# Column-half matmuls kept together in groups, and the second batch mixed row by row for all token groups, in a scheduled attention and token-mixing kernel

## Chip, cores and metric

The kernel runs on one core of one Trainium2 chip. The metric is the device time of one execution in microseconds (us). Three executions of the kernel before took 296.97, 297.04 and 297.30 us; the median, 297.04 us, is the time to compare with. The profile comes from one more execution, of 297.23 us, and its span (first to last instruction) is 295.5 us.

## What is computed

The reference has two parts. A polynomial-sketch attention over 4 batches, 4 heads, 1088 tokens and 32 dimensions a head, and then a token-mixing block on the result, laid out as 4 batches of 1088 tokens with 128 features.

```python
def phi(x):                                   # S1, S2: 8 x 32
    a = einsum('rd,bhsd->bhsr', S1, x); b = einsum('rd,bhsd->bhsr', S2, x)
    return outer product of a and b, 64 features for a token and head
q_p, k_p = phi(q), phi(k)
kv  = einsum('bhsf,bhsd->bhfd', k_p, v)       # 64 x 32 for each head
z   = sum of k_p over the tokens
num = einsum('bhsf,bhfd->bhsd', q_p, kv)
den = einsum('bhsf,bhf->bhs', q_p, z) + 1e-6
x = num / den, heads side by side             # (batch, token, 128)

theta = x @ w_theta
zr, zi = x * cos(theta), x * sin(theta)
y = w_tok_r @ zr + w_tok_i @ zi               # over tokens: 1088 x 1088, for each batch
u = x + y
out = u + relu(u @ w_ch)
```

The denominators can come close to zero, so the kernel computes them in slices of numbers that add up exactly (the names `ksl`, `qsl`, `mv`, `lv`, `cut_r`, `cut_z`, `fl` belong to that). The features, `kv`, the numerators and the mixing run on 32-bit floats. The mixing weights come as 64-bit floats and are turned into 32-bit ones on the chip, in 34 pieces (`w_tok` into `st`, then `step` and `wT`).

## The kernel before

The kernel does not call the engines directly. It records each instruction (`note`), with an estimated duration and the earlier instructions that it must follow; at the end `lay_out` goes through a list schedule and issues everything in the order found. Among the instructions of an engine that could start within `WAIT` of the earliest, the one with the smallest `due` is taken. `due` runs back from the mixing matmuls, which get `START[b]` plus a pace, and is shifted for each stage by `SOONER[stage]`. So these constants decide the order on each engine, and the order is fixed when the program is built. Each engine then executes its own list in that order.

```python
START = 101.9, 134.2, 165.1, 246.3
SOONER = {"denominators0": 4.5, "denominators1": -11, ...}     # cut: 49 stages
PACE = 2.9
...
class Order:
    WAIT = 0.08
    ...
    def note(self, engine, fn, call, a, kw):
        ...
        op = Operation(engine, fn, a, kw, len(self.ops), cost, late, self.due)
        op.stage = self.stage
        ...                                    # cut: whom it must follow
        self.ops.append(op)
        return op
    ...
    def lay_out(self):
        ...                                    # cut: the list schedule fills `out`
        for op in out:
            r = [x.real() if isinstance(x, View) else x for x in op.args]
            op.call(*r, **{k: x.real() if isinstance(x, View) else x for k, x in op.kw.items()})
```

PSUM is one pool of 8 buffers of 512 floats a partition, all under the name `w`. Tokens come in 9 chunks of 128 (the last one half filled), and in 3 groups of 3 chunks (`NG = 3`, `GC = 3`). Two places use matmuls whose output has only 64 partitions: a pair of heads gives the columns 0 to 63 of the array, the other pair the columns 64 to 127.

```python
def keys_values(b):                            # feat: features of the keys; big: the values
    vn = tiles["v", b]
    kv = psum()[:, :P]
    for g in range(NG):
        ks = tiles["kf", b, g]
        kp = buf("feat", [P, CH, R, R], F32, 2)
        tt(V, kp, ...)                         # the outer product, on VectorE
        for i in range(GC):
            for n in range(2):
                c = g * GC + i
                T.matmul(kv[n * 2 * D:(n + 1) * 2 * D], vn[:, c, 2 * n:2 * n + 2]...,
                         kp[:, i * H + 2 * n:i * H + 2 * n + 2]...,
                         start=(c == 0), stop=(c == NC - 1),
                         tile_position=(0, n * 2 * D), skip_group_check=True)
    ...                                        # cut: kv is put into kvbd

def numerator(b, g):
    ...                                        # cut: features of the queries, transposed into fT
    xp = psum()[:, :GC * P]
    for n in range(2):
        T.matmul(xp[n * 2 * D:(n + 1) * 2 * D], kvbd[b % 2][:, n], qpT[n],
                 start=True, stop=True, tile_position=(0, n * 2 * D), skip_group_check=True)
    return xp
```

The mixing of a batch adds up 17 products for each group of tokens: 8 chunks of `zr`, 8 of `zi`, and one that holds the two half chunks. The first batch goes row by row: each of the 17 weight rows is used for the three groups at once, as the weights arrive. The other batches go group by group.

```python
rows = [j * NF + i for i in range(NF) for j in range(2)] + [NK - 1]

def mix_sums(b, gs, yps):
    zr, zi, zl = tiles["z", b]
    for n, i in enumerate(rows):
        z = zr[:, i] if i < NF else zi[:, i - NF] if i < NK - 1 else zl
        for g, yp in zip(gs, yps):
            t0, t1 = g * GC * P, min((g + 1) * GC * P, S)
            order.due = START[b] + (PACE * n if len(gs) > 1 else 0.65 * (g * NK + n))
            T.matmul(yp[:, :t1 - t0], z, wT[:, i, t0:t1], start=(n == 0), stop=(n == NK - 1))

def mixing(b):
    for gs in (range(NG),) if b == 0 else ((g,) for g in range(NG)):
        yps = [psum() for _ in gs]
        order.stage = f"mixing{b}"
        mix_sums(b, gs, yps)
        for g, yp in zip(gs, yps):
            mix_out(b, g, yp)                  # add x, the channel matmul, transpose, store
    order.due = math.inf
```

Of the kernel before, what the change touches and what calls it, by code (L numbers as in the profile page):

```python
# [36 lines left out]
ROUND = 1.5 * 2.0**23  # L37
TWO_PI = 6.2831850
TINY = 2.0**-60
START = 101.9, 134.2, 165.1, 246.3  # L40
BIG = 5

SOONER = {"denominators0": 4.5, "denominators1": -11, "denominators2": -106, "denominators3": -89,
          "features0": 23, "features1": 45.5, "features2": -47.5, "features3": 32.5,
          "keyfeatures0": 25, "keyfeatures1": 16.5, "keyfeatures2": 20.5, "keyfeatures3": 67.5,
          "keys1": 45.5, "keys2": -14.5, "keys3": -30.5, "matrix0": 9, "matrix1": 36.5,
          "matrix2": 6.5, "matrix3": 55.5, "mixed00": -8.5, "mixed01": 24.5, "mixed02": -0.5,
          "mixed10": -5, "mixed11": -13, "mixed12": 31, "mixed20": 190, "mixed21": -53,
          "mixed22": 66, "mixed30": 51, "mixed31": 24, "mixed32": -22, "mixing0": -53,
          "mixing1": -66, "mixing2": -52, "mixing3": -24, "out0": -43, "out1": -30, "out2": -26,  # L50
          "out3": 109, "slices0": 3.5, "slices1": -9, "slices2": -72, "slices3": -20, "values0": 5,
          "values1": 39.5, "values2": 28.5, "values3": 17.5}
ST = 6
PACE = 2.9
PIECE = 544


# [54 lines left out]

class Operation:
    def __init__(self, engine, call, args, kw, n, cost, late, due):
        self.engine, self.call, self.args, self.kw, self.n = engine, call, args, kw, n
        self.cost, self.late, self.due = cost, late, due
        self.behind, self.bufs = [], []

# [22 lines left out]
class Order:  # L141
# [3 lines left out]

    WAIT = 0.08

    def __init__(self, nc):  # L150
        self.nc, self.ops, self.due, self.tags, self.stage = nc, [], math.inf, {}, None
        self.dve, self.act = self.Engine(self, "DVE", nc.vector), self.Engine(self, "ACT", nc.scalar)
        self.pe, self.sp = self.Engine(self, "PE", nc.tensor), self.Engine(self, "SP", nc.sync)

# [22 lines left out]
    def duration(self, engine, call, out, ins):  # L177

        n = math.prod(out.shape[1:])
        psum = any(isinstance(x, View) and x.buf.tag == "w" for x in ins)  # L180
        if engine == "DVE":
            if call == "tensor_reduce":
                n = math.prod(ins[0].shape[1:])
            if call == "reciprocal":
                return 0.29, 0.1
            own = any(isinstance(x, View) and x.shape[1:] == (1,) for x in ins[1:])
            fast = call in ("tensor_scalar", "tensor_copy", "memset") and not psum
            return 0.09 + n / (1920 if fast and not own else 1400 if fast else 970), 0.1
        if engine == "ACT":
            wide = any(isinstance(x, View) and x.buf.tag == "st" for x in ins)  # L190
            own = any(isinstance(x, View) and x.shape[1:] == (1,) for x in ins[1:])
            return 0.05 + 0.07 * own + n / (900 if out.dtype != F32 and wide else 1020 if wide else 1130), 0.15
        if engine == "SP":
            return 0.36, 0.0
        if call == "transpose":
            return 0.11, 0.3
        if ins[0].dtype == F32:
            return (n / 1200 + 0.03 if ins[0].shape[1] == 64 else max(0.22, n / 600)), 0.3
        return max(0.06, n / 2400), 0.3

    def note(self, engine, fn, call, a, kw):
        names = [k for k in ("out", "dst") if k in kw]
        out = kw[names[0]] if names else a[0]
        ins = [x for x in [*a, *kw.values()] if x is not out and hasattr(x, "rearrange")]
        cost, late = self.duration(engine, call, out, ins)
        op = Operation(engine, fn, a, kw, len(self.ops), cost, late, self.due)
        op.stage = self.stage
        if engine == "PE":
            passes = 2 if call == "transpose" else 4 if ins[0].dtype == F32 else 1
            op.stream = min(cost, math.prod(out.shape[1:]) * passes / 2400)  # L210
        if engine == "SP":
            op.bytes = math.prod(out.shape) * mybir.dt.size(out.dtype)
        behind = set()
        for x, write in [(x, False) for x in ins] + [(out, True)]:
            if not isinstance(x, View):
                continue
            b = x.buf
            p0, p1, b0, b1 = box = x.box()
            for n, w, (q0, q1, c0, c1) in b.seen:
                if (w or write) and p0 < q1 and q0 < p1 and b0 < c1 and c0 < b1:  # L220
                    behind.add(n)
            if write and engine == "PE":
                if b.pe is not None:
                    behind.add(b.pe)
                b.pe = op.n
            b.seen.append((op.n, write, box))
            if not b.uses or b.uses[-1] != op.n:
                b.uses.append(op.n)
                op.bufs.append(b)
        behind.discard(op.n)  # L230
        op.behind = sorted(behind)
        self.ops.append(op)
        return op

    def dues(self):
# [7 lines left out]
    def lay_out(self):  # L243
# [49 lines left out]
        while len(self.log) < len(ops):  # L293
# [21 lines left out]
            t, op = best  # L315
# [24 lines left out]
                if not left[n]:  # L340
                    ready[o.engine].append(o)
        for op in out:
            r = [x.real() if isinstance(x, View) else x for x in op.args]
            op.call(*r, **{k: x.real() if isinstance(x, View) else x for k, x in op.kw.items()})  # L344


@with_exitstack
def kernel(
# [12 lines left out]
    B, _, NC, H, D = q.shape  # L361
# [4 lines left out]
    NK = 2 * NF + 1  # L366
    GC = 3
    NG = NC // GC
# [334 lines left out]
    def keys_values(b):  # L703
# [5 lines that stand above are left out]
            kp = buf("feat", [P, CH, R, R], F32, 2)  # L709
            tt(V, kp, ks[:, :, 0:R].unsqueeze(3).to_broadcast([P, CH, R, R]),  # L710
               ks[:, :, R:2 * R].unsqueeze(2).to_broadcast([P, CH, R, R]), ALU.mult)
            for i in range(GC):
                for n in range(2):
                    c = g * GC + i

                    T.matmul(kv[n * 2 * D:(n + 1) * 2 * D], vn[:, c, 2 * n:2 * n + 2].rearrange("p h d -> p (h d)"),
                             kp[:, i * H + 2 * n:i * H + 2 * n + 2].rearrange("p h i j -> p (h i j)"),
                             start=(c == 0), stop=(c == NC - 1), tile_position=(0, n * 2 * D), skip_group_check=True)
        kvt = buf("kvt", [P, P])
        A.copy(kvt, kv)  # L720
        t = psum()[:, :P]
        T.transpose(t, kvt, ident)
        t = t.rearrange("p (n d) -> p n d", n=2)
        for j in range(2):
            pj = slice(j * R * R, (j + 1) * R * R)
            A.copy(kvbd[b % 2][pj, :, j * D:(j + 1) * D], t[pj, :, j * D:(j + 1) * D])
# [90 lines left out]
    def numerator(b, g):  # L817
        fl = tiles["fl", b].rearrange("p t (n r) -> p t n r", r=R)[:, :, g * CH:(g + 1) * CH]
        qp = buf("feat", [P, CH, R, R], F32, 2)
        tt(V, qp, fl[:, 1].unsqueeze(3).to_broadcast([P, CH, R, R]),  # L820
           fl[:, 0].unsqueeze(2).to_broadcast([P, CH, R, R]), ALU.mult)
        qpT = [buf("fT", [P, GC * P], F32, 4) for _ in range(2)]
        for n in range(2):
            tr = psum()
            for i in range(GC):
                T.transpose(tr[:, i * P:(i + 1) * P],
                            qp[:, i * H + 2 * n:i * H + 2 * n + 2].rearrange("p h i j -> p (h i j)"), ident)
            A.copy(qpT[n], tr[:, :GC * P])
        xp = psum()[:, :GC * P]
        for n in range(2):  # L830

            T.matmul(xp[n * 2 * D:(n + 1) * 2 * D], kvbd[b % 2][:, n], qpT[n],
                     start=True, stop=True, tile_position=(0, n * 2 * D), skip_group_check=True)
        return xp

    def mixed(b, g, xp):
# [36 lines left out]
# [3 lines that stand above are left out]
            z = zr[:, i] if i < NF else zi[:, i - NF] if i < NK - 1 else zl  # L876
            for g, yp in zip(gs, yps):
                t0, t1 = g * GC * P, min((g + 1) * GC * P, S)
                order.due = START[b] + (PACE * n if len(gs) > 1 else 0.65 * (g * NK + n))
                T.matmul(yp[:, :t1 - t0], z, wT[:, i, t0:t1], start=(n == 0), stop=(n == NK - 1))  # L880

    def mix_out(b, g, yp):
# [29 lines left out]

    def mixing(b):

        for gs in (range(NG),) if b == 0 else ((g,) for g in range(NG)):
            yps = [psum() for _ in gs]
            order.stage = f"mixing{b}"
            mix_sums(b, gs, yps)
# [132 lines left out]
```

## Time and profile before

| | |
|---|---|
| time, median of three | 297.04 us |
| span of the profile | 295.5 us, 3773 instructions |
| TensorE matmul (PE) | 257.6 us busy, 87% |
| VectorE (DVE) | 224.8 us, 76% |
| ScalarE (ACT) | 166.0 us, 56% |
| mean granted TensorE clock | 0.912 |
| read from and written to memory | 28.5 MB, 97 GB/s over the span |

The same, by stretches of time (busy us of each engine, and the granted TensorE clock in that stretch):

| stretch, us | PE | DVE | ACT | clock |
|---|---|---|---|---|
| 0 to 20 | 7.65 | 15.87 | 12.51 | 0.87 |
| 20 to 77 | 37.15 | 55.87 | 45.10 | 0.71 |
| 77 to 140 | 62.49 | 58.85 | 52.74 | 0.90 |
| 140 to 152 | 11.84 | 11.21 | 11.59 | 1.00 |
| 152 to 290 | 137.39 | 82.50 | 43.49 | 1.00 |
| 290 to 296 | 1.05 | 0.49 | 0.53 | 0.91 |

How to read the names: every instruction is issued from the same line of the recording layer (L344), so groups are told apart by their tiles. `w<-wT,st` is a mixing matmul, `w<-feat,big` one of `keys_values` and `w<-fT,kvbd` one of `numerator`; `128*64` means a weight operand of 64 columns. A matmul on 32-bit floats leaves two records in the trace, a transpose or a 16-bit matmul one. The records of one engine overlap: a matmul's record ends after the next one has begun. The room that a matmul takes is therefore read from its start to the start of the next one, not from its length.

### The profile page before, as it was taken

How to read it: one execution, taken by the hardware profiler on the slowest of the kernel's cores; microseconds unless marked ns; L12 is line 12 of the kernel's file. 1: busy time of each engine (PE TensorE's matmuls, PEld its weight loads, DVE VectorE, ACT ScalarE, POOL GpSimd, SP SyncE). 2: the span in 40 equal slices, each digit the busy share in tenths (PEclk: the TensorE clock that was granted, in tenths of full speed). 3: DMA queues.
4: the chain of work that ended last, by engine and by line, in shares of the span. 5: the costliest groups of instructions: out<-in, count | busy, mean ns of one | idle time of the engine just before them, and what ended most of it. 6: DMA issues, size and time to landing. Idle time of an engine off the chain costs nothing.

```text
span 295.5 us, 3773 instructions
## 1 busy us (share of the span) xinstructions
PE 257.6 (87%) x1255; PEld 168.1 (57%) x1255; DVE 224.8 (76%) x638; ACT 166.0 (56%) x326; POOL 0.7 (0%) x6
## 2 busy tenths in 40 slices
PE   4539584945599999999999999999999999999993
PEld 3426553524477656656565545677656666665671
DVE  5999999999998999979999447999881994421011
ACT  3696579999528999789992223226734004620000
POOL 0000000000000000000000000000000000000000
PEclk9957867775559999999999999999999999999999
DMA  7999115967002166753300000110000001000010
GB/s 252 384 355 353 21 67 201 332 239 226 0 0 83 31 205 220 223 151 106 131 1 27 27 2 0 41 36 1 23 2 0 27 0 29 22 0 0 27 29 22
DMA packets 11603, 28.77 MB, mean 97 GB/s; under 512 B 1216, under 2 KB 5568, under 8 KB 11584
## 3 DMA queue, kind: packets, MB, share of 16 engines
q1 hardware_dynamic: 11584, 28.53, 28.7%
q8 instruction: 10, 0.16, 0.2%
q14 instruction: 9, 0.07, 0.1%
HBM read 26.30 MB, written 2.23 MB: 97 GB/s over the span
## 4 chain that ended last, share of the span: by engine, by line
PE 74%; DVE 15%; ACT 7%; DMA 1%; issue 1%; ACTq 0%
PE w L344 74%; ACT step L344 3%; DVE big L344 2%; DVE wT L344 2%; DVE lv L344 2%; DMA big<-k_l 1%; ACT big L344 1%; DVE cut_r L344 1%; DVE ksl L344 1%; DVE feat L344 1%; ACT lv L344 1%; ACT wT L344 1%; ACT tn L344 1%; DVE cut_z L344 1%; ACT fT L344 1%
## 5 line engine op out<-in xcount | busy, mean ns | idle before, releaser
L344 PE MATMUL w<-wT,st 128*128 128x384 f32 (+1 forms) x384 | 130.9, 473 | 0.0
L344 PEld LDWEIGHTS w<-wT,st 128*128 128x128 f32 x384 | 68.3, 190 | 36.9 <-issue 5.2
L344 ACT ACTIVATE step<-st 128x544 f16<-128x544 f32 (+2 forms) x70 | 54.4, 827 | 5.7 <-DVE wT L344 5.6
L344 ACT COPY ot<-w 128x384 f32<-128x384 f32 (+2 forms) x16 | 6.0, 394 | 62.6 <-PE w L344 50.4
L344 DVE TENSOR_TENSOR uT<-xT,w 128x384 f32<-128x384 f32 (+1 forms) x12 | 6.4, 530 | 28.0 <-PE w L344 27.9
L344 PE MATMUL w<-feat,big 128*64 128x128 f32 x144 | 18.3, 325 | 7.5 <-DVE feat L344 7.5
L344 DVE CUSTOM_DVE_ANT_0 wT<-wT,step 128x1088 uint16<-128x1088 uint16 x34 | 24.3, 719 | 0.7 <-ACT step L344 0.3
L344 ACT ACTIVATE wT<-st 128x544 f32<-128x544 f32 x34 | 23.6, 713 | 0.4 <-DMA st<-w_tok 0.4
L344 ACT COPY fT<-w 128x384 f32<-128x384 f32 x36 | 16.2, 490 | 9.9 <-PE w L344 9.9
L344 ACT COPY lv<-w 128x384 f32<-128x384 f32 x36 | 16.1, 500 | 8.3 <-PE w L344 8.0
L344 PEld LDWEIGHTS w<-feat,big 128*64 128x64 f32 x144 | 11.1, 156 | 15.1 <-DVE feat L344 8.2
L344 PE MATMUL w<-ident,big 128*128 128x128 f32 x72 | 13.8, 346 | 6.7 <-ACT big L344 4.2
L344 PE MATMUL w<-s_bd,fT 128*128 128x64 f32 x72 | 13.7, 353 | 6.1 <-DVE s_bd L344 6.1
L344 PE MATMUL w<-mv,qsl 128*128 128x384 f16 (+2 forms) x108 | 16.2, 290 | 1.6 <-ACT lv L344 1.3
L344 PEld LDWEIGHTS w<-s_bd,fT 128*128 128x128 f32 x72 | 12.7, 264 | 6.9 <-DVE s_bd L344 6.2
L344 PEld LDWEIGHTS w<-ident,big 128*128 128x128 f32 x72 | 11.5, 185 | 8.4 <-ACT big L344 4.6
L344 DVE TENSOR_SCALAR wT<-wT 128x544 int32<-128x544 int32 x34 | 14.5, 435 | 0.4 <-ACT wT L344 0.3
L344 PE MATMUL w<-ksl 128*128 128x384 f16 x72 | 14.6, 362 | 0.0
L344 PEld LDWEIGHTS <-qsl 128*128 128x128 f16 x108 | 9.9, 99 | 7.8 <-issue 4.5
L344 PE MATMUL w<-fT,kvbd 128*64 128x384 f32 x48 | 13.3, 542 | 0.2 <-ACT fT L344 0.2
L344 DVE SCALAR_TENSOR_TENSOR tt<-tn,w 128x384 f32<-128x384 f32 x12 | 6.6, 552 | 8.6 <-ACT tn L344 8.4
L344 PE MATMUL w<-ident,feat 128*128 128x128 f32 x72 | 12.9, 302 | 0.3 <-ACT big L344 0.3
(190 smaller groups left out, 402.1 us busy)
## 6 DMA issues: line engine op xcount, KB each, us to landing
st<-w_tok SPq DMA_DIRECT2D x34, 544.0 KB, 4.9
big<-k_l SPq DMA_DIRECT2D x4, 576.0 KB, 4.9
big<-q_l SPq DMA_DIRECT2D x4, 576.0 KB, 3.9
big<-v_l SPq DMA_DIRECT2D x4, 576.0 KB, 5.4
out<-ot SPq DMA_DIRECT2D x8, 192.0 KB, 2.1
out<-ot SPq DMA_DIRECT2D x4, 128.0 KB, 1.8
st<-w_sq SPq DMA_DIRECT2D x1, 256.0 KB, 4.9
out<-ot SPq DMA_DIRECT2D x4, 32.0 KB, 1.8
```

The lines of the kernel that those rows point to most:

```text
L344: op.call(*r, **{k: x.real() if isinstance(x, View) else x for k, x in op.kw.items()})
```

## The change

The change keeps certain instructions together and then sets the scheduler's constants anew.

- `together` makes one operation of all that is recorded inside it. Its parts are issued one after the other with nothing between them, under one estimated cost. It is used for the 6 half matmuls of one group in `keys_values`, and for the 2 of `numerator`, so that instructions on columns 0 to 63 and 64 to 127 alternate and no instruction of another kind stands between them.
- The second batch (`b == 1`) is mixed like the first, row by row for the three groups of tokens, and no longer group by group.
- `START`, `SOONER`, `PACE` and `WAIT` are new, and so are some estimates of `duration`. These are numbers of the scheduler alone, but through them nearly the whole order changes on all engines.

What is computed stays the same. The built program has the same 856 matmul instructions of the same shapes on TensorE as before, and the same number of instructions on VectorE and ScalarE; only their order and the buffers they use differ.

```diff
-START = 101.9, 134.2, 165.1, 246.3
+START = 118, 121.6, 209.9, 242.1
-SOONER = {"denominators0": 4.5, "denominators1": -11, ...}
+SOONER = {"denominators0": 43.5, "denominators1": -128, ...}      # cut: all stages are new
-PACE = 2.9
+PACE = 1.6
-    WAIT = 0.08
+    WAIT = 0.03
...
-            return (n / 1200 + 0.03 if ins[0].shape[1] == 64 else max(0.22, n / 600)), 0.3
+            return max(0.22, n / 600), 0.3
+    @contextmanager
+    def together(self, cost):
+        self.joined = []
+        yield
+        op, self.joined = self.joined[0], None
+        op.cost = cost
...                                            # cut: note() adds to the joined operation
-            op.call(*r, **{k: x.real() if isinstance(x, View) else x for k, x in op.kw.items()})
+            for call, args, kw in op.parts:
+                r = [x.real() if isinstance(x, View) else x for x in args]
+                call(*r, **{k: x.real() if isinstance(x, View) else x for k, x in kw.items()})
...                                            # keys_values
-            for i in range(GC):
-                for n in range(2):
-                    T.matmul(kv[...], ...)
+            with order.together(0.81):
+                for i in range(GC):
+                    for n in range(2):
+                        T.matmul(kv[...], ...)
...                                            # numerator
-        for n in range(2):
-            T.matmul(xp[...], ...)
+        with order.together(0.85):
+            for n in range(2):
+                T.matmul(xp[...], ...)
...                                            # mix_sums
-                order.due = START[b] + (PACE * n if len(gs) > 1 else 0.65 * (g * NK + n))
+                order.due = START[b] + (PACE if b == 0 else 1.95) * n if len(gs) > 1 else START[b] + 0.65 * (g * NK + n)
...                                            # mixing
-        for gs in (range(NG),) if b == 0 else ((g,) for g in range(NG)):
+        for gs in (range(NG),) if b < 2 else ((g,) for g in range(NG)):
```

## The prediction, made before the changed kernel ran

> **What bounds the kernel now.** I read the page from the top: busy times, the span in slices, the chain of waits, then the groups.
>
> ```profile
> PE 257.6 (87%) x1255; PEld 168.1 (57%) x1255; DVE 224.8 (76%) x638; ACT 166.0 (56%) x326; POOL 0.7 (0%) x6
> ...
> PE   4539584945599999999999999999999999999993
> ...
> DVE  5999999999998999979999447999881994421011
> ACT  3696579999528999789992223226734004620000
> ...
> PEclk9957867775559999999999999999999999999999
> ...
> PE 74%; DVE 15%; ACT 7%; DMA 1%; issue 1%; ACTq 0%
> ...
> L344 PE MATMUL w<-feat,big 128*64 128x128 f32 x144 | 18.3, 325 | 7.5 <-DVE feat L344 7.5
> L344 PE MATMUL w<-fT,kvbd 128*64 128x384 f32 x48 | 13.3, 542 | 0.2 <-ACT fT L344 0.2
> ```
>
> A slice is 7.4 us. Up to slice 10 (77 us) VectorE is full and TensorE has holes at a low clock; from there TensorE is full to the end, and the chain is 74% TensorE. VectorE stays nearly full to slice 20 (150 us): it converts the mixing weights beside its other work. So there are three stages: VectorE sets 20 to 77 us; from 77 to about 152 us both are full; from 152 us TensorE alone sets the pace (137.39 of 138 us busy, VectorE 82.50).
>
> Next the timeline of TensorE, for what a column-half matmul costs by its neighbours:
>
> ```profile
> 51.59 0.88 PE L344 MATMUL w<-feat,big 128*64 128x128 f32 x12 [2.52 <-DVE feat L344]
> 52.40 0.96 PE L344 MATMUL w<-ksl 128*128 128x384 f16 x3
> ...
> 128.16 0.86 PE L344 MATMUL w<-fT,kvbd 128*64 128x384 f32 x2
> 128.96 0.83 PE L344 MATMUL w<-ksl 128*128 128x256 f16 x5
> ...
> 174.40 0.43 PE L344 MATMUL w<-feat,big 128*64 128x128 f32 x2
> 174.76 0.27 PE L344 MATMUL w<-ident,m 128*8 128x128 f32 x1
> 174.97 0.43 PE L344 MATMUL w<-feat,big 128*64 128x128 f32 x2
> 175.33 0.91 PE L344 MATMUL w<-wT,st 128*128 128x384 f32 x2
> 176.17 0.43 PE L344 MATMUL w<-feat,big 128*64 128x128 f32 x2
> ...
> 209.54 0.87 PE L344 MATMUL w<-fT,kvbd 128*64 128x384 f32 x4
> 210.34 0.18 PE L344 MATMUL w<-sz,cz 128*128 128x16 f16 x1
> ```
>
> Take starts, not lengths. Six key matmuls in one run (12 records) take 51.59 to 52.40: 0.81 us, 0.135 each. One alone (2 records) takes 174.97 to 175.33: 0.36. The mixing matmul behind it takes 175.33 to 176.17, 0.84, where 0.645 is usual between its own kind: of those 0.19 us, 0.10 follow the half matmul before it and 0.09 precede the next one. One numerator matmul takes 0.80 (128.16 to 128.96), and two together also 0.80 (209.54 to 210.34).
>
> **What the Trainium skill says.** "TensorE: Matmul & The Clock Gate", section Part 3: Packing small matmuls, says that outputs on distinct column strips run at once; the trace agrees, two numerator matmuls in the 0.80 us of one. "TensorEngine Tiling (Array Packing)", section Key Properties, says "Mode switching requires drain": going from whole array to halves empties TensorE. The trace agrees with the 0.09 us before and about 0.10 us behind a run. "Perfetto Trace Analysis", section Identifying the Most-Contended Engine, warns that matmul busy share is no measure of TensorE's room; hence I sum start-to-start steps.
>
> **The change, part by part.**
>
> *Halves together.* Only runs after 77 us count, where TensorE is full. Batch 2's key matmuls (91 to 100.5 us) come in 8 runs of 1 to 3 instructions: their steps sum to 3.75 us, plus 8 entries x 0.09 = 4.5. As 3 whole groups: 3 x (0.81 + 0.09) = 2.7; **1.8 saved**. Batch 3's (162 to 181 us) come in 12 runs among mixing matmuls: 4.8, plus 12 x 0.09, plus about 9 exits into mixing x 0.10 = 6.8; whole: 2.7 + 3 x 0.10 = 3.0; **3.8 saved**. Four numerator matmuls ran alone (128 to 143 us), each 0.80 + 0.09; as two pairs they cost half: **1.8 saved**. The sum is 7.4 us. Nothing is added: the 856 matmuls are the same.
>
> *The order.* The order of the built instructions of both programs is known. I gave each TensorE instruction its full-clock step from the trace (0.645 us for 384 mixing columns, 0.538 for 320, 0.109 a transpose, runs of halves as above) and summed along each order: 230.5 us before, 222.3 after, **8.2 less**. Against the trace, the clock time is this sum plus an offset: 52.5 at the first numerator (86.0 us), 54.4 at 91 us, 55.9 at 152 us, 59.3 at the end. The offset grows by cold clock, idle time and small extra steps; it hardly grows after 90 us, so the sum is a fair ruler.
>
> Likewise for VectorE, mean step of each kind of instruction. Before, it has done 79 us of work at the first query product (83 us); in the new order 81 us stand ahead of it. So the first numerator comes about 2 us later, at 88 us, with 33.1 us of TensorE work ahead of it (before 33.4): offset 55, and 57 after the cold start that before too cost 2 us.
>
> *Mixing batch 1 by rows.* It adds no matmul. It lets this mixing start as soon as the first tokens' `z` are there. In the new order mixing of batch 0 ends at TensorE sum 80 (before 99), batch 1 starts at 90 and ends at 129.
>
> *Where VectorE holds it.* The last row of batch 0's mixing needs the last weights. Before, VectorE had 143 us of work ahead of the end of the last conversion, which ended at 151.4 us; in the new order 133. VectorE had done 133 at 140.1 us. ScalarE's share: its last weight copy ends at its work sum of 112.9, before 120.4 (150.3 us); at 113 it stood near 142 us. So the last weights come at about **141 us**. TensorE's sum is 79 there, so the offset is 62, not 57: TensorE must wait some 4 to 5 us between 120 and 141. Batch 1's first `z` says the same: 144.7 of VectorE work, about 152 us, with TensorE at 90: offset 62. Before, at 152 us, TensorE's sum was 96 of 230.5, leaving 134.5; after it is 90 of 222.3, leaving 132.3. From there the offset grew by 3.4 before, of which I take off about 1.2 for batch 3's fragments: 2.2. End: 222.3 + 62 + 2.2 = 286.5, before 230.5 + 59.3 = 289.8. **3.3 us less**: 297.04 - 3.3 = 293.7. I say 293.4, as order and scheduler were tuned together and a little of the wait may go.
>
> **The rivals.**
>
> *A. TensorE stays the bound all through.* Then offset 57 at 91 us plus 4 gives 222.3 + 61 = 283.3, 6.5 less, 290.5 us. For it: before, TensorE waited only 0.4 us between 86 and 290 us. Against it: VectorE has 58.85 of 63 us busy from 77 to 140 us, and the new order leaves TensorE less other work to put in while weights arrive.
>
> *B. The gain is lost ahead of 77 us.* The order there is new too. VectorE's chain to the first denominators has 64 us of work ahead instead of 62, and a lost handshake between VectorE, ScalarE and TensorE costs 1 to 4 us (before, one wait for `ACT big` was 4.22 us). All later work shifts: 294 to 297.
>
> *C. PSUM runs short.* Three buffers of 8 are held by batch 1's mixing from sum 90 to 129, where one was held before. Work of batches 2 and 3 must go through 5. Batch 0 was mixed with three held and TensorE did not starve (0 idle from 90 to 126 us), so I give this little: 295 if it bites.
>
> *D. A late chain.* The denominators of batch 3 must be done between features (sum 159) and numerators (178) : 19 us, as before (167 to 186), where it just fitted. Slack of 3 to 4 us for batch 2 (113 to 131). A miss costs 1 to 3 us.
>
> **Range and chances.** The middle is 293.4. A brings it to 290.5, B to D to 295 to 297; ordered engines can go wrong in small ways that only a run shows. Range 289.0 to 296.8. 2% faster is 291.1: it needs nearly all of A, chance 0.26. Slower by 2% (303) would need 10 us of new waits: 0.04. The rest, 0.70, lies within 2%.
>
> **What would show it.** The timeline after must show `w<-feat,big` in 12s and `w<-fT,kvbd` in 4s, their steps near 0.81 and 0.80: else the 7.4 us are wrong. TensorE's idle time between 100 and 145 us, waiting for VectorE `wT` or `st`, should be 4 to 6 us; if it is under 1, A holds. The last weight conversion should end near 141 us, the first numerator start near 88. After 152 us TensorE should have under 2 us idle; waits there for `fT`, `z` or a PSUM buffer would speak for C or D. The prediction fails if VectorE reaches 133 us of work clearly before 138 or after 145 us.

## The result and the profile after

| | before | after |
|---|---|---|
| time, median (lowest to highest) | 297.14 us (296.97 to 297.30) | 292.16 us (291.87 to 292.38) |
| ratio, with its 95% interval | 1 | 0.983 (0.9815 to 0.9849) |
| span of the profile | 295.5 us | 290.1 us |
| mean granted TensorE clock | 0.912 | 0.903 |

The changed kernel is 1.7% faster: inside the range and within 2%, 1.2 us under the figure of the prediction. The page of the kernel after, in the order in which the prediction read the page before (busy times, slices, chain, and the group of half matmuls that is among its costliest):

```profile
PE 248.8 (86%) x1255; PEld 165.2 (57%) x1255; DVE 225.6 (78%) x638; ACT 163.5 (56%) x326; POOL 0.7 (0%) x6
...
PE   4699857470049999999999999999999999999993
...
DVE  5999899999999999998999669989862993511011
ACT  3598759999039999999567082037704004710000
...
PEclk9957955865557999999999999999999999999998
...
PE 70%; DVE 20%; ACT 6%; DMA 1%; issue 1%; ACTq 0%
...
L361 PE MATMUL w<-feat,big 128*64 128x128 f32 x144 | 10.5, 281 | 1.8 <-DVE feat L361 1.8
```

The key matmuls fell from 18.3 to 10.5 us busy. Two slices of TensorE (65 to 80 us) and one of ScalarE (72 to 80 us) are now empty; behind them TensorE is full to the end. The timeline of TensorE shows the halves in whole groups (start, length, then what runs; the step to the next start is the cost):

```profile
104.16 0.88 PE L361 MATMUL w<-feat,big 128*64 128x128 f32 x12
104.97 2.20 PE L361 MATMUL w<-wT,st 128*128 128x384 f32 x6
...
137.99 1.99 PE L361 MATMUL w<-wT,z 128*128 128x384 f32 x6
...
142.31 0.87 PE L361 MATMUL w<-fT,kvbd 128*64 128x384 f32 x4
143.10 0.33 PE L361 MATMUL w<-ident,feat 128*128 128x128 f32 x1
```

Six key matmuls take 104.97 - 104.16 = 0.81 us, two numerators 0.79. All key matmuls stand in 12 records and all numerators in 4. No line of this view from 99 to 284 us carries a wait. The stretches of the prediction, for the kernel after (PE, PEld, DVE and ACT busy, then the clock):

```profile
77.00:140.00 63.00, 56.12 (x276) 36.60 (x277) 61.13 (x129) 54.21 (x101) 0.00 (x0) 0.89 0.47 162
140.00:152.00 12.00, 12.00 (x79) 8.29 (x79) 11.83 (x24) 7.45 (x18) 0.00 (x0) 1.00 0.18 48
```

TensorE lost 6.4 us of busy time from 77 to 140 us (56.12 for 62.49): 5.65 us of that is idle time ahead of 82.65 us. VectorE gained 2.3 (61.13 for 58.85). With the prediction's ruler, the sum of TensorE's full-clock steps against the clock time:

| | before | predicted | after |
|---|---|---|---|
| sum of the whole order, us | 230.5 | 222.3 | 222.3 |
| first numerator, us | 86.0 | 88 | 90.8 |
| offset (clock time less sum) near 91 us | 54.4 | 57 | 57.7 |
| offset where the last weights are used | 55.9 (152 us) | 62 (141 us) | 59.4 (138 us) |
| offset at the end | 59.3 | 64.2 | 62.2 |
| end = sum + offset | 289.8 | 286.5 | 284.5 |

So 8.2 us of TensorE's order were saved, and 2.9 us came back as offset.

### The profile page after: what moved, and what is told of

Same layout as the page of the kernel before. It is cut to its first block, busy times and chain, and to the rows that moved or that the text cites. A ratio compares the mean times of both kernels' runs of the same rounds, so it can differ in the third digit from the quotient of the medians.

```text
span 290.1 us, 3786 instructions
## 1 busy us (share of the span) xinstructions
PE 248.8 (86%) x1255; PEld 165.2 (57%) x1255; DVE 225.6 (78%) x638; ACT 163.5 (56%) x326; POOL 0.7 (0%) x6
## 4 chain that ended last, share of the span: by engine, by line
PE 70%; DVE 20%; ACT 6%; DMA 1%; issue 1%; ACTq 0%
PE w L361 70%; DVE wT L361 4%; DVE big L361 3%; DVE lv L361 2%; ACT step L361 1%; DMA big<-k_l 1%; DVE cut_r L361 1%; ACT lv L361 1%; ACT fT L361 1%; ACT tn L361 1%; DVE cut_z L361 1%; ACT qsl L361 1%; DVE dn L361 1%; DVE feat L361 1%; DVE fl L361 1%
## 5 line engine op out<-in xcount | busy, mean ns | idle before, releaser
L361 PE MATMUL w<-wT,st 128*128 128x384 f32 (+1 forms) x384 | 125.4, 472 | 0.0
L361 PEld LDWEIGHTS w<-wT,st 128*128 128x128 f32 x384 | 70.0, 190 | 38.4 <-issue 1.6
L361 ACT COPY fT<-w 128x384 f32<-128x384 f32 x36 | 16.9, 491 | 36.1 <-PE w L361 35.9
L361 PE MATMUL w<-mv,qsl 128*128 128x288 f16 (+2 forms) x108 | 20.2, 341 | 0.3 <-DVE mv L361 0.3
L361 PEld LDWEIGHTS w<-ident,big 128*128 128x128 f32 x72 | 10.8, 177 | 14.2 <-issue 8.5
L361 PEld LDWEIGHTS <-qsl 128*128 128x128 f16 x108 | 12.0, 116 | 7.6 <-issue 3.9
L361 ACT ACTIVATE big<-big,ipk 128x288 f32<-128x288 f32 x16 | 8.3, 531 | 12.3 <-DVE ipk L361 9.4
L361 DVE TENSOR_REDUCE m<-big 128x4 f32<-128x1152 f32 x8 | 10.7, 1346 | 2.4 <-DMA big<-k_l 2.4
L361 PE MATMUL w<-feat,big 128*64 128x128 f32 x144 | 10.5, 281 | 1.8 <-DVE feat L361 1.8
L361 PEld LDWEIGHTS w<-ident,feat 128*128 128x128 f32 x72 | 9.0, 149 | 5.3 <-DVE feat L361 1.8
```

## Experiments: which part of the change pays

Theory T: only the sum of TensorE's steps counts, because TensorE waits for nothing from 91 us on. Theory V, the prediction's: VectorE's weight conversions hold it near 140 us. A third reading, R: the new constants, not the halves, bring the gain. Ratios are to the kernel before, timed again beside each set of runs (medians from 296.85 to 297.14 us); differences of less than about half a microsecond between the times of two versions are given no meaning.

**Halves gathered in the order of before.** The scheduler of before runs unchanged; the half matmuls of a group are then issued together, at the place of the last of them.

```diff
+        for op in out:                     # out: the order of before
+            if op.group is None: moved.append(op); continue
+            held.setdefault(op.group, []).append(op)
+            if last[op.group] == op.n: moved += held.pop(op.group)
```

> The order of before on every engine, constants and mixing of before too; only the half matmuls of one group (6 key matmuls, 2 numerator matmuls) are issued together, at the place where the last of them stood. TensorE's summed steps fall from 230.5 to 222.8 us, like those of the changed kernel (222.3). Theory T (TensorE is the bound from about 90 us on, and the saving in halves is the whole gain): 289 to 290 us, as the better start of before (offset 54.4 against 57.7 at 91 us) stays. Theory V (the last mixing weights, which here end on VectorE at 151 us as before, hold TensorE once it has less to do): TensorE waits 2 to 4 us between 140 and 152 us, 291 to 293 us. Theory R (the new order and the mixing by rows made the gain, not the halves): 296 to 297 us.

Measured: 291.72 us (291.06 to 292.80), ratio 0.980 (0.9753 to 0.9848). From its TensorE timeline (in brackets the idle time before, and who ended it):

```profile
98.34 0.88 PE L375 MATMUL w<-feat,big 128*64 128x128 f32 x12
99.15 0.54 PE L375 MATMUL w<-mv,qsl 128*128 128x384 f16 x3
...
140.82 0.18 PE L375 MATMUL w<-sz,cz 128*128 128x8 f16 x1 [0.40 <-DVE cz L375]
```

TensorE's sum is 222.8, 7.7 less than before; the offset is 56.0 at 101 us, 58.0 at 154, 60.9 at the end. Gathering alone gives the whole gain; R falls. T's figure of 289 to 290 was too low, since of the 7.7 us about 2 came back as offset. The time lies in V's band, but V's wait did not come: from 140 to 152 us TensorE waited 0.40 us, and not for weights. The time of the changed kernel lies inside this run's spread, so its new constants and its rows add nothing that these runs can tell.

**Halves apart in the changed kernel.** `together` no longer joins, so that the scheduler orders the halves singly.

```diff
-        self.joined = []
         yield
-        op, self.joined = self.joined[0], None
-        op.cost = cost
```

> The changed kernel with all its constants and the mixing of batch 1 by rows, but the halves are not kept together; the scheduler then finds another order, with 12 runs of 1 to 3 key matmuls and 8 lone numerator matmuls. TensorE's summed steps are 228.6 us against 222.3. Theory T: slower than the changed kernel by 5 to 7 us, 297 to 299 us. Theory R: within 1.5 us of the changed kernel, 291 to 293.5 us.

Measured: 319.76 us (318.88 to 320.15), ratio 1.074 (1.0679 to 1.0792). The sum is 228.6, 6.3 above the changed kernel's, but the time rose by 27.6. The waits of TensorE tell where the rest is (tile and engine waited for: total, times, longest):

```profile
PE w L358 <- ACT ks L358: 10.2, 1, 10.2
PE w L358 <- DVE feat L358: 9.2, 4, 4.4
PE w L358 <- DVE uT L358: 4.1, 6, 0.9
```

The constants were set for joined operations, and without them the scheduler found another order. The time lies outside both bands. So this run does not measure the halves; it shows that an edit of the program ahead of such a scheduler edits everything.

**Batch 1 by groups again, ordered anew.**

```diff
-        for gs in (range(NG),) if b < 2 else ((g,) for g in range(NG)):
+        for gs in (range(NG),) if b == 0 else ((g,) for g in range(NG)):
```

> The changed kernel, but batch 1 is mixed group by group as before. TensorE's summed steps are the same (222.6 us). Theory T: within 1.5 us of the changed kernel, 291 to 293.5 us, as TensorE finds other work. Theory R (the rows are what lets TensorE run while weights arrive): waits of TensorE of 2 to 5 us between 100 and 150 us, 294 to 297 us.

Measured: 302.61 us (301.05 to 304.33), ratio 1.016 (1.01 to 1.0227). The sum is 222.6, as after; two waits ahead of 85 us, 10.0 for `feat` and 9.4 for `mv`, and one of 2.8 for `wT` at 140 us are new. In this order, then, TensorE does wait for weights. Again it is the order that was measured. From here on, therefore, orders were kept and single places exchanged.

**Batch 1 by groups, in the same places.** The order of all engines is the changed kernel's; the 51 places of batch 1's mixing matmuls are filled group by group.

```diff
+        places = [i for i, o in enumerate(pe) if o is a mixing matmul of batch 1]
+        for i, o in zip(places, sorted((pe[i] for i in places), key=group and row)):
+            pe[i] = o
```

> The changed kernel, all orders kept, but the 51 places that batch 1's mixing has in TensorE's order are filled group by group in place of row by row. TensorE's work is the same (222.3 us). Group by group, the seventh matmul already needs z of the second group of tokens and the thirteenth that of the third, which VectorE has ready at about 155 and 159 us; TensorE is there at 155 and 160 us. Theory T: at most 1.5 us slower than the changed kernel, 292 to 294 us. Theory R (rows are what keeps TensorE fed): 3 us or more slower, 295 us or more.

Measured: 293.39 us (293.17 to 293.76), ratio 0.988 (0.9855 to 0.9901), 1.2 us above the changed kernel. One wait is new in the timeline of TensorE:

```profile
156.28 0.91 PE L393 MATMUL w<-wT,st 128*128 128x384 f32 x2 [0.69 <-DVE st L393]
```

A later group's `z` is asked for before VectorE has it. So the rows are worth this 0.7 us within this order, and 1.2 at most: the first numerator already came 0.5 us later (91.24 for 90.77), ahead of all that was edited.

**Halves in column order.** In the changed kernel, three matmuls on columns 0 to 63, then three on 64 to 127, instead of alternating. They still stand together.

```diff
-                for i in range(GC):
-                    for n in range(2):
+                for n in range(2):
+                    for i in range(GC):
```

> The changed kernel; within each kept-together group of six key matmuls the three on columns 0 to 63 come first and the three on columns 64 to 127 after, where they alternated. No other instruction moves. If running at once on the two halves is what the group gains, a group takes 6 x 0.218 + 0.15 = 1.46 us for 0.81; six groups lie where TensorE is full, so 6 x 0.65 = 3.9 us more, 295 to 296.5 us. If the gain is only that TensorE is emptied less often, nothing changes: 292 us.

Measured: 294.53 us (294.49 to 294.73), ratio 0.989 (0.9852 to 0.9933), 2.4 us above the changed kernel. Its TensorE timeline:

```profile
105.04 1.15 PE L361 MATMUL w<-feat,big 128*64 128x128 f32 x12
106.11 2.20 PE L361 MATMUL w<-wT,st 128*128 128x384 f32 x6
...
114.14 1.14 PE L361 MATMUL w<-feat,big 128*64 128x128 f32 x12
115.21 1.18 PE L361 MATMUL w<-wT,st 128*128 128x384 f32 x3
```

A group takes 1.07 us instead of 0.81. That lies between the two outcomes expected, 1.46 and 0.81: in column order the halves overlap only in part. Six of the twelve groups lie where TensorE is full, and 6 x 0.26 makes 1.6 us of the 2.4. The rest was lost before them: the first of the six starts at 105.04 us for 104.16, and what lost it is not shown. So alternating is a real part of the gain. That matmuls on distinct column strips run at once is what the Trainium skill says ("TensorE: Matmul & The Clock Gate", Part 3: Packing small matmuls); the trace agrees, and adds that it depends on the order in which they are issued.

**Two groups joined.** The gathered kernel of the first run, with the second group's key matmuls moved to the third's in each batch, to save entries into the half mode.

```diff
+        for b in range(4):
+            ops = the key matmuls of batch b, group 1
+            pe[i:i] = ops               # i: place of group 2's first
```

> The gathered version of before (its order, halves of a group together), and in each batch the six key matmuls of the second group of tokens moved on to stand directly ahead of those of the third, so that TensorE changes to halves once for both. TensorE's summed steps are 221.8 us for 222.8; half of the saving lies where TensorE is full. Theory T: 0.4 to 0.8 us faster than the gathered version, about 291 us; a wait of VectorE for a feature buffer would take it back.

Measured: 292.94 us (291.74 to 293.29), ratio 0.986 (0.9825 to 0.9885). The sum fell by 1.0 to 221.8, the offset at the end rose from 60.9 to 63.6. Of that 0.7 us stands already at the first numerator (86.67 us for 85.93), and small waits follow, such as 0.42 us for `dgr` at 173 us and three for `lv` from 96 to 99. No gain, then: the sum fell, and waits took it back. Which of them the moved matmuls caused is not shown.

## Experiments: what sets the two holds

**The last weights.** In the changed kernel, 20 of the 34 VectorE shifts of the weight conversion are left out, those from 86.87 us on (8.8 us of VectorE); the output's values become other ones.

```diff
+            if op is a shift of wT and not among the first 14: continue
```

> The changed kernel with every order kept, without the last 20 of the 34 shifts (VectorE, between 84 and 132 us of its work): 20 x 0.44 = 8.8 us less for VectorE while weights arrive, so that the last weights come some 6 to 9 us sooner. Theory T (TensorE is full from 100 us on and waits for no weights): at most 0.7 us faster, 291.4 to 292.5 us. Theory V of the prediction (the weights hold TensorE before 141 us): 3 us or more faster, 289 us or less.

Measured: 291.85 us (291.40 to 292.30), ratio 0.983 (0.98 to 0.985): 0.3 us from the changed kernel, inside the spread. But the weights did not come 6 to 9 us sooner. The last conversion as VectorE's timeline shows it, in the kernel after and in this run (the second of each pair), and the longest item of the waits of VectorE in this run (total, times, longest):

```profile
136.74 1.36 DVE L361 CUSTOM_DVE_ANT_0 wT<-wT,step 128x1088 uint16<-128x1088 uint16 x2
```

```profile
136.43 1.38 DVE L365 CUSTOM_DVE_ANT_0 wT<-wT,step 128x1088 uint16<-128x1088 uint16 x2 [0.47 <-ACT step L365]
```

```profile
DVE wT L365 <- ACT step L365: 5.1, 7, 1.7
```

The stretch from 100 to 138 us (PE, PEld, DVE and ACT busy) in the kernel after, then in this run:

```profile
100.00:138.00 38.00, 38.00 (x179) 24.58 (x178) 36.42 (x73) 37.56 (x67) 0.00 (x0) 1.00 0.56 192
```

```profile
100.00:138.00 38.00, 38.00 (x180) 24.83 (x179) 31.80 (x59) 37.55 (x67) 0.00 (x0) 1.00 0.56 192
```

In this run the last conversion ends at 137.8 us, for 138.1 in the kernel after. Relieved of 8.8 us, VectorE waited 5.1 us (between 84 and 139 us) for ScalarE's step copies, and ScalarE was as full as before. So VectorE's load does not set when the last weights come, and that part of theory V falls; the run does not test weights that come earlier. That TensorE does not wait for them is read from the kernel after itself: from 100 to 138 us it is busy for 38.00 of 38 us, and no wait stands in its timeline. It begins the last row of batch 0 at 137.99 us (the `w<-wT,z` line above), 0.5 us after the first of the two conversions has ended (137.46), and reaches the columns of the second, which ends at 138.1, at 138.64. The room is half a microsecond.

**The front, VectorE.** The first 14 shifts are left out instead (6.1 us of VectorE, the last of them at 64.06 us).

```diff
+            if op is a shift of wT and among the first 14: continue
```

> The changed kernel with every order kept, without the first 14 of the 34 shifts in the conversion of the mixing weights (VectorE, 0.44 us each, all within its first 60 us of work); those weights come out wrong in value, nothing else is left out. It takes 14 x 0.44 = 6.1 us from VectorE ahead of the first numerator. If VectorE's work sets when TensorE becomes full, the offset of TensorE at 100 us falls from 58.7 to 53 to 55 and the time to 286 to 288.5 us. If it is ScalarE or the round trips between engines that set it, the time falls by under 2 us.

Measured: 292.18 us (291.25 to 293.38), ratio 0.985 (0.9817 to 0.9883); first query product of VectorE at 83.83 us for 84.50, first numerator at 90.2 for 90.8. Of 6.1 us, 0.7 arrived. VectorE now waits between 60 and 70 us (busy for 8.54 of 10), where ScalarE is busy for 10.00 of 10.

**The front, ScalarE, and both.** The first 14 of ScalarE's copies that make the low half of a weight's step are left out (9.7 us), alone, and together with the 14 shifts. GpSimd fills the step buffers with zeros at the start. The output's last digits change in the one, its values in the other.

```diff
+        for x in the three step buffers: gpsimd.memset(x, 0.0)
+            if op is a low half and among the first 14: continue
+            if op is a shift of wT and among the first 14: continue     # second run only
```

> The changed kernel without the first 14 of the 34 ScalarE copies that make the low half of a weight's step (0.69 us each, 9.7 us of ScalarE, most of them between 40 and 75 us); the three step buffers are filled with zeros by GpSimd at the start. What is left out makes the output's last digits other ones. From 40 to 70 us ScalarE is busy without a gap and VectorE waits for its lv and step copies. Theory 'ScalarE alone sets the front': the first feat product of VectorE comes 3 us or more earlier than 84.5 us and the time falls by 2 us or more, to 290 or less. Theory 'ScalarE and VectorE are both full there, one without the other gives little': the front moves by under 1.5 us and the time by under 1 us: 291.2 to 292.2.

> The two left out together: the first 14 low halves on ScalarE (9.7 us) and the first 14 shifts on VectorE (6.1 us); step buffers filled with zeros at the start. What is left out makes the output's values other ones. Theory 'both are full': now the first feat product comes 4 to 6 us before 84.5 us, the first numerator near 86 us, and the time falls by 3 to 5 us, to 287 to 289, though neither alone gave 1 us. Theory 'TensorE and the DMA of the keys hold the front': the first numerator still comes at 89 us or later and the time falls by under 2 us.

Measured: 292.24 us (291.92 to 292.57), ratio 0.985 (0.9829 to 0.9862), first numerator at 90.4; and 291.55 us (290.08 to 292.24), ratio 0.981 (0.9787 to 0.9838), at 90.5. In the traces, taking 9.7 us from one engine and 6.1 from the other moves the first numerator by 0.3 us. The trace of the last run is of an execution of 292.13 us, one of its slower ones; its fastest, 290.08, is still above the 287 to 289 that I expected. My favoured theory, that both engines are full there and only both together give, is wrong. The timelines of the four kernels show a fixed series instead: batch 0's feature matmuls (`w<-mv,qsl`) start as soon as VectorE has `mv`, at 58.36 us after, 57.65 without the shifts, 58.14 without the low halves and 58.95 without both; VectorE's first step on their results (`fl<-lv`) follows 9.8, 9.8, 9.8 and 9.5 us later; and from 70 to 84 us VectorE is busy for 13.99 of 14 us in all four. This suggests that the work left out lies beside this series. What sets the 9.8 us and the moment of `mv` itself was not tried.

**The hole in ScalarE.** The timelines of TensorE and ScalarE after show two holes that belong together:

```profile
82.65 0.87 PE L361 MATMUL w<-ident,big 128*128 128x128 f32 x3 [8.48 <-DMA big<-k_l]
...
90.77 0.87 PE L361 MATMUL w<-fT,kvbd 128*64 128x384 f32 x4
```

```profile
83.56 0.48 ACT L361 COPY fT<-w 128x384 f32<-128x384 f32 x1 [10.86 <-PE w L361]
```

The keys of batch 2 arrive at 82.65 us, TensorE stands in front of their transposes, and ScalarE in front of the copy of those. Here two step copies are moved ahead of that copy, on ScalarE alone, into exchanged step buffers.

```diff
-  ACT: fT, qsl, step, lv, step, lv, ...
+  ACT: step, step, fT, qsl, lv, lv, ...
```

> The changed kernel, in which ScalarE makes two of its step copies (the two of one weight tile, 0.69 us each) ahead of the fT copy at 83.56 us, in front of which it stands idle for 10.86 us, instead of behind it; the two step buffers concerned change places. Nothing else moves. Theory 'ScalarE holds the first numerators': behind 84.6 us ScalarE is full (qsl, step, lv and fT copies without a gap), so the first fT copies and the first numerator come up to 1.4 us earlier (89.4 us for 90.8), and the program ends 1.0 to 1.4 us earlier: about 291. Rival 'TensorE holds them': between 85.5 and 90.8 us TensorE has work without a gap too, at a low clock, so the numerator comes under 0.5 us earlier and the time stays at 292.

Measured: 296.30 us (295.78 to 297.84), ratio 0.997 (0.9952 to 0.999): 4.1 us slower than the changed kernel. ScalarE's timeline shows the mistake, TensorE's its effect:

```profile
86.97 1.47 ACT L400 ACTIVATE step<-st 128x544 f16<-128x544 f32 x2 [14.37 <-DVE wT L400]
...
89.88 0.50 PE L400 MATMUL w<-mv,qsl 128*128 128x192 f16 x2 [3.70 <-ACT qsl L400]
```

No step buffer was free: VectorE empties one at 86.9 us, behind its long series. I had taken the edit for free because the hole was. The failed edit still measures something: the `qsl` copy came 4.0 us late, the first numerator 3.1, TensorE's offset at the end is 65.9 for 62.2, and the time 4.1 us longer. A delay here is not absorbed later.

**Both holes filled.** Six step copies go into ScalarE's hole, written into the last columns of `wT`, which no weight has reached yet; 24 matmuls of the identity with itself, whose result is overwritten, fill TensorE's.

```diff
-  ACT: fT, qsl, step, lv, step, lv, step, lv, fT, ...
+  ACT: step x6 (into wT), fT, qsl, lv, lv, lv, fT, ...
+  PE:  24 x matmul(w, ident, ident) ahead of the transposes of `big`
```

> The changed kernel with the two idle stretches ahead of 83 us filled. ScalarE: the next six step copies (0.69 us each) stand ahead of the fT copy before which it idled 10.86 us; they go into the last columns of wT, which no weight has reached yet, so that no step buffer has to come free[...]. TensorE: 24 matmuls of the identity with itself, whose result is overwritten, stand ahead of the key transposes before which it idled 8.48 us, so that it comes to them at a high clock. The order of all else is kept. Theory 'ScalarE's step copies and the low clock hold the first numerators together': three step copies, 2.1 us, go from ahead of the second fT copy, and TensorE's 5.3 us from 85.5 to 90.8 us shrink by 2 or more; the first numerator starts at 88 to 88.8 us instead of 90.8, and since the run before showed that a shift there reaches the end in full, the time is 289.5 to 290.5. Rival 'VectorE holds them' (it is full from 60 to 92 us, and the second feat product of batch 0's queries stands behind weight additions): the numerator comes less than 0.7 us earlier, 291.5 to 292.3. Third outcome: the weight buffers released early bring their transfers into the way of k_l, which lands later than 82.65 us, and the time rises above 292.5.

Measured: 292.55 us (292.12 to 292.94), ratio 0.984 (0.9812 to 0.9873): no gain. From its TensorE timeline:

```profile
84.11 0.55 PE L408 MATMUL w<-ident,big 128*128 128x128 f32 x3 [2.13 <-DMA big<-k_l]
...
90.14 0.87 PE L408 MATMUL w<-fT,kvbd 128*64 128x384 f32 x4
...
95.98 0.44 PE L408 MATMUL w<-ident,big 128*128 128x128 f32 x2 [1.09 <-DVE tt L408]
99.96 1.48 PE L408 MATMUL w<-wT,st 128*128 128x384 f32 x4
```

The keys arrive 1.4 us later (84.11 for 82.65), as the third outcome had it (whether for its reason is not shown), but behind them TensorE waits for VectorE's `feat` up to 85.85 us, so this costs nothing. The numerator starts 0.6 us earlier all the same, and then TensorE waits 1.09 us for VectorE's `tt`, which it did not wait for before; the mixing run that follows starts at 99.96 us, in the kernel after at 99.80. The rival was right in its cause, the time 0.25 us above its band: with ScalarE and TensorE relieved, VectorE, full there, holds the same moment. Its product `feat` for batch 0's queries starts at 84.84 us for 84.50, and `tt` at 95.37 for 95.03, the same 10.53 us behind it in both kernels. The clock helped only briefly, as two stretches show (the clock is the third number from the end):

```profile
84.10:85.20 1.10, 1.09 (x7) 0.67 (x7) 1.10 (x2) 0.50 (x2) 0.00 (x0) 1.00 0.04 16
85.80:87.50 1.70, 1.65 (x8) 1.17 (x9) 1.70 (x3) 1.20 (x3) 0.00 (x0) 0.50 0.20 27
```

No version beat the changed kernel by more than the spread of its own runs.

## Why the prediction was nearly right, step by step

- **Halves together, 7.4 us.** Right, in its units (0.81 and 0.79 us measured) and as a sum: gathering alone took 7.7 us from TensorE's order, and that run has the changed kernel's time within its spread.
- **The order's sum, 222.3.** Known beforehand, and a fair ruler: behind 99 us the offset grew by 3.5 us only, up to the end.
- **First numerator at 88 us, offset 57 at 91.** It came at 90.8, but at full clock, where I had added 2 us of low clock behind it. The offset is 57.7: two errors, of +2.8 us and about -2, nearly cancel, which is luck. I had followed VectorE alone (its first query product came at 84.50 us, as late as its own work said) and not ScalarE's and TensorE's holes and the low clock behind them.
- **VectorE holds TensorE near 141 us, 4 to 5 us.** This is the step that failed, and the mis-sized term. The offset grew from 57.7 to 59.4 by 138 us, 1.7 us instead of 5, and most of that ahead of 100 us; TensorE's idle time from 100 to 145 us is none. By the prediction's own test (under 1 us), rival A holds. The last conversion ended at 138.1 us, not near 141: VectorE had lost 5.1 us against its 133 us of work, where I took the 7 that it had lost before. That lies at the edge of the prediction's other test ("clearly before 138"). The cause was wrong as well as the size: with 8.8 us of VectorE's work left out, the last weights still came at 137.8 us, as VectorE then waited for ScalarE.
- **Drift to the end, 2.2 us.** 2.8 measured (59.4 to 62.2).
- Together, against the predicted offsets: 0.7 more at 91 us, 3.3 less of a hold (1.7 for 5), 0.6 more drift. That is 2.0 us less, and the end is at 284.5 for 286.5; 0.3 us of it I had granted in the figure of 293.4. So the figure came near although the wait that it counted on did not occur. That it came so near is in part luck: the front and the drift cost 1.3 us more than forecast.
- **The rivals.** A (TensorE bound all through) describes the picture from 99 us on, but its size, 6.5 us less, was too large: 5.3 in the trace. Of the 1.2 us between them, 0.7 stands at 91 us and 0.5 behind it. Rival B, the front, did cost: 2.7 us of offset at 101 us against the gathered run with the order of before (58.7 for 56.0), most of which the forecast had as 57 for 54.4 at 91 us. C and D did not show: behind 152 us TensorE's timeline has no wait but two of 0.58 us for `uT` at the very end.

## What to carry to other kernels

Matmuls that use half of the array's columns belong together, alternating, with nothing between them; that alone was worth 2.0% here (1.5 to 2.5), and it can be done by gathering them in an existing order without retuning anything. To size it, sum start-to-start steps over the built order of the bound engine, and hold a second engine's arrival as a wait only if its time is later than the bound engine's own by more than the error of both: here a forecast of 141 us was off by 3 us, and the weights came half a microsecond before they were needed. When leaving work out is meant to bring something forward, see first whether it came: here the next full engine, ScalarE, held the weights at the same time. When a scheduler stands between the source and the order, test a part of a change by exchanging places in the finished order; two runs that let it order anew measured only the new order.

## What the runs showed of the hardware, unexpected

- Column halves issued in column order overlap in part: six key matmuls take 1.07 us, where 0.81 is alternating and six times one alone among whole-width matmuls (0.36) would be 2.16.
- A key group directly ahead of two numerators costs less: in the timeline after, it starts at 200.17 us, they at 200.88 and what follows at 201.63, so 0.71 and 0.75 us instead of 0.81 and 0.80. No whole-width matmul stands between them; that a change of mode saved is the reason is not shown.
- The clock went from half to full 4.1 us after the first of the 24 filling matmuls (74.45 us; steps from record to record of 0.213 us, then 0.112). "TensorE: Matmul & The Clock Gate", Part 1: The HAM clock gate, speaks of about 3.4 us of sustained work, in a window that runs freely, so that the moment varies by 0.5 us; here it was 0.7 us longer than 3.4. It was still full at 84.1 to 85.2 us behind an idle 2.1 us, and half again at 85.8, behind 1.1 us of work and 0.62 more of idle time.
